# Half of wo with w_mod's FFN part ahead of the last K, w1 apart, w2 in five pieces, and a store of 128 partitions

## The chip, the core and the metric

The kernel runs on one core of one Trainium2 chip. The core has five engines that run their own instruction streams and meet through semaphores: PE (TensorE, matrix products; weight loads into it are shown apart as PEld), DVE (VectorE), ACT (ScalarE), POOL (GpSimd) and SP (SyncE), which here issues every DMA. The DMA engines move data between the chip's main memory and the on-chip memory (SBUF, 128 partitions); PE writes into PSUM, which also has 128 partitions.

The metric is the device time of one execution in microseconds (us), and the median over several runs. The profile is of one execution; its span runs from the first to the last instruction.

## What is computed

One decode step of a transformer block with conditioning, for a batch of 4, width 512, 32 query heads on 8 key/value heads ("groups", so 4 heads share a group), a window of 2048 cached positions, head size 128, and an FFN of width 1792. All values are 32-bit floats.

```python
def _A_ref(x, k_cache, v_cache, wq, wo):
    q = (x @ wq) ...
    k = jnp.repeat(k_cache[:, :, Sk - W:, :], rep, axis=1)
    v = jnp.repeat(v_cache[:, :, Sk - W:, :], rep, axis=1)
    scores = jnp.einsum("bhqd,bhkd->bhqk", q, k) * (Dh ** -0.5)
    p = _softmax(scores, axis=-1)
    o = jnp.einsum("bhqk,bhkd->bhqd", p, v)
    return o.transpose(0, 2, 1, 3).reshape(B, Sq, Hq * Dh) @ wo

def _B_ref(x, w1, w3, w2):
    return (_silu(x @ w1) * (x @ w3)) @ w2

mod = (_silu(c) @ w_mod).reshape(c.shape[0], 6, 1, -1)
sa, ca, ga, sb, cb, gb = ...
h = _layernorm(x) * (1 + ca) + sa
x = x + ga * _A_ref(h, A_k_cache, A_v_cache, A_wq, A_wo)
h = _layernorm(x) * (1 + cb) + sb
x = x + gb * _B_ref(h, B_w1, B_w3, B_w2)
```

Each of the eight groups needs 4 MB of K and 4 MB of V; the weights are wq and wo with 8 MB each, w_mod with 6 MB, and w1, w3 and w2 with 3.5 MB each. Every byte is used once.

## The kernel before

**Order and waits.** The function `block_kernel` lists all operations in one order. The class `Program` (lines 42 to 138) records each, works out from the places that it touches which earlier operations it has to wait for, and gives each engine its own part of that order with the waits as semaphores. An engine runs its part strictly in order. Every instruction is emitted on line 52, so the profile's line numbers don't tell them apart; the names of the tiles do. `do.mark()` splits the list in two parts with separate semaphores.

**The ring.** `ring` is one buffer of three slots of 8 MB (`slots[0]` to `slots[2]`), each of two halves of `HALF` = 8192 values for each partition (4 MB). All large loads go into it, in this order: w_mod's two attention columns (`w_mod_a`, slot 0), `xc_in` (x and c), wq (slot 1), then K and V of groups 0 to 7 in turn (`kv_in[g]`, 8 MB each, K in a slot's first half and V in its second), with wo (8 MB, slot 0) between group 6 and group 7. Group 7 comes as two loads, K and V, in slot 1. Then follow `w_mod_b` (slot 2: the four other columns of w_mod, 4 MB, and w1 behind them in the same load), w3 (slot 1, first half, in place of K7) and w2 (slot 1, second half, in place of V7) in four pieces, cut at chunks 0, 8, 12, 13 and 14 (`W2_CUTS`). The function `load` issues each on SP, which waits until the slot's former contents have been read.

**A group** (`group`, lines 306 to 326): PE multiplies the queries with K into four PSUM tiles `s_ps`; DVE takes the maximum of each (`mx`, then `nm`); PE turns the former group's output (`heads_out(g-1)`, tile `o_sb` times `pick`, into `oT`); ACT takes the exponent (`p_sb`), PE transposes it, DVE copies it to `pT`, PE multiplies it with V into `o_ps`; ACT scales it to `o_sb`.

**The end** (lines 338 to 403). After group 6, `project_out(0)` to `project_out(5)` multiply the finished heads with wo into `a_ps`; each call is four matmuls. Then comes group 7, `project_out(6)`, `heads_out(7)` and `project_out(7)`. ACT copies `a_ps` to `work`, and PE sums it into `attn`. `mod_columns` (16 matmuls of silu(c) with w_mod's four FFN columns) gives `mod_b`, which holds `ga`, `sh`, `cb1` and `gb`. DVE computes x1 = x + `ga` * `attn`; `norm` and `modulate` give h, which is transposed to `h2T`. `ffn_in` multiplies it with w1 (the gate, into `s_ps[0]`) and then with w3 (up, into `s_ps[1]`); each is 16 matmuls, a copy and four transposes. The product `hidT` meets w2 in 14 chunks of four matmuls, of which the last stands behind the mark. DVE multiplies with `gb` and adds x1 into `res`. Values for the four batch rows stand in every eighth partition, so the store takes `res[::8, :]`: 16 rows of 512 bytes.

Of the kernel before, what the change touches and what calls it, by code (L numbers as in the profile page):

```python
# [3 lines left out]
F32 = mybir.dt.float32  # L4
# [4 lines left out]
B, D, HQ, G, SK, DH, W, FF = 4, 512, 32, 8, 8192, 128, 2048, 1792  # L9
P = 128  # L10
R = HQ // G
# [1 line left out]
NC = 4  # L13
CHUNKS = [(c, j) for c in range(4) for j in range(4 if c < 2 else 3)]
NF = len(CHUNKS)
W2_CUTS = [0, 8, 12, 13, 14]
EPS = 1e-5
HALF = 8192

# [118 lines left out]
                nc.sync.sem_clear(done)  # L138


def block_kernel(nc, xc_in, w_mod_a, wq, kv_in, wo, w_mod_b, w3, w2, out):

# [1 line left out]
    do = Program(nc)  # L146

    def sb(name, *shape):
        return nc.alloc_sbuf_tensor(name, (P, *shape), F32).ap()

    def ps(name):
        return nc.alloc_psum_tensor(name, (P, 512), F32).ap()

    ring = sb("ring", 6 * HALF)
    slots = [ring[:, n * 2 * HALF : (n + 1) * 2 * HALF] for n in range(3)]
    s_ps = [ps(f"s_ps{t}") for t in range(NT)]
    banks = [ps(f"bank{n}") for n in range(2)]
    a_ps, o_ps = ps("a_ps"), ps("o_ps")
    turn = [0]

    def bank():
        turn[0] += 1
        return banks[turn[0] % 2]

    def load(dst, src):
        do("sync", "dma_start", dst, src)
        return dst

    def batch(t):

# [4 lines left out]
    x_sb, ct_sb = xc_sb[:, :P], xc_sb[:, P:]  # L175


    wma = load(slots[0][:, : w_mod_a.shape[1]], w_mod_a)
    load(xc_sb, xc_in)
    wq_t = load(slots[1], wq)  # L180
    kv = [None] * G
    kv[0] = load(slots[2], kv_in[0])
# [27 lines left out]
    oT = sb("oT", G, R, B)  # L210
# [9 lines left out]
    ss, ln, r0, ve, a, r = (sb(n, 1) for n in ("ss", "ln", "r0", "ve", "a", "r"))  # L220
# [26 lines left out]
    def mod_columns(wv, dst, n):  # L247

        pb = bank()
        for k in range(4):  # L250
            for j in range(4):
                do("tensor", "matmul", pb[32 * j : 32 * j + 32, : n * P], sc[:, k, :], wv[:, k, j, :], start=(k == 0), stop=(k == 3))
        do("vector", "tensor_copy", dst, pb[:, : n * P])
# [21 lines left out]
    for half in range(2):  # L275
# [4 lines left out]
        for i in range(R):  # L280
            src = qtp[:, i * P : (i + 1) * P].rearrange("p (g q) -> p g q", g=4)[:, :, ::8]
# [7 lines left out]

    def project_out(g):  # L290
        for i in range(R):
            do("tensor", "matmul", a_ps[32 * i : 32 * i + B, :], oT[:, g, i, :], wo_t[:, g, i, :], start=(g == 0), stop=(g == G - 1))

    mx, nm, ls, l, rl = (sb(n, m) for n, m in (("mx", NT), ("nm", 1), ("ls", NT), ("l", 1), ("rl", 1)))
    p_sb = [sb(f"p_sb{t}", 512) for t in range(NT)]
# [10 lines left out]
    def group(g):  # L306
        kt, vt = (kv[g][:, i * HALF : (i + 1) * HALF].rearrange("p (t b n) -> p t b n", t=NT, b=B) for i in range(2))
        for t in range(NT):
            for b in range(B):
                do("tensor", "matmul", s_ps[t][32 * b : 32 * b + 32, :], qT[:, g, b, :], kt[:, t, b, :], start=True, stop=True)  # L310
            do("vector", "reduce_max", mx[:, t : t + 1], s_ps[t], axis=AX.X)
        do("vector", "tensor_reduce", nm, mx, axis=AX.X, op=ALU.max, negate=True)
        if g:
            heads_out(g - 1)
        for t in range(NT):
            do("scalar", "activation", p_sb[t], s_ps[t], AF.Exp, bias=nm, accum_out=ls[:, t : t + 1])
            pt = bank()
            for c in range(NC):
                do("tensor", "transpose", pt[:, c * P : (c + 1) * P], p_sb[t][:, c * P : (c + 1) * P], ident)
            do("vector", "tensor_copy", pT[t], pt.rearrange("p (c b i) -> p b c i", b=B, i=32)[:, :, :, :R])  # L320
            for u in [t - 1] * (t > 0) + [t] * (t == NT - 1):
                for b in range(B):
                    do("tensor", "matmul", o_ps[32 * b : 32 * b + NC * R, :], pT[u][:, b].rearrange("p c r -> p (c r)"), vt[:, u, b, :], start=(u == 0), stop=(u == NT - 1))
        do("vector", "reduce_sum", l, ls, axis=AX.X)
        do("vector", "reciprocal", rl, l)
        do("scalar", "activation", o_sb, o_ps, AF.Copy, scale=rl)

    for g in range(G - 1):
        group(g)
        if g < 4:  # L330
            kv[g + 3] = load(slots[(g + 2) % 3], kv_in[g + 3])
        elif g == 4:
            wo_t = load(slots[0], wo).rearrange("p (g r n) -> p g r n", g=G, r=R)
        elif g == 5:
            kv[7] = slots[1]
            for i in range(2):
                load(kv[7][:, i * HALF : (i + 1) * HALF], kv_in[7][:, i * HALF : (i + 1) * HALF])
    wmb = load(slots[2][:, : w_mod_b.shape[1]], w_mod_b)
    for g in range(G - 2):
        project_out(g)  # L340
    group(G - 1)
    w3_t = load(slots[1][:, : w3.shape[1]], w3)
    w2_t = slots[1][:, HALF : HALF + w2.shape[1]]
    step = w2.shape[1] // NF
    for lo, hi in zip(W2_CUTS[:-1], W2_CUTS[1:]):
        load(w2_t[:, lo * step : hi * step], w2[:, lo * step : hi * step])
    project_out(G - 2)
    heads_out(G - 1)
    project_out(G - 1)

    do("scalar", "copy", work, a_ps)
    attn = bank()
    for j in range(4):
        do("tensor", "matmul", attn[32 * j : 32 * j + 32, :P], spread, work[:, j * P : (j + 1) * P], start=True, stop=True)

    mod_b = sb("mod_b", 512)
    ga, sh, cb1, gb = (mod_b[:, i * P : (i + 1) * P] for i in range(4))
    mod_columns(wmb[:, : 4 * 4 * 512].rearrange("p (k j i) -> p k j i", k=4, j=4), mod_b, 4)
    do("vector", "tensor_scalar_add", cb1, cb1, 1.0)
    x1, ag, tot2 = sb("x1", P), sq, sb("tot2", 1)  # L360
    do("vector", "tensor_mul", ag, attn[:, :P], ga)
    do("vector", "scalar_tensor_tensor", x1, ag, 1.0, x_sb, op0=ALU.mult, op1=ALU.add, accum_out=tot2)
# [4 lines left out]
    def ffn_in(ws, pg, g_sb):  # L367

        ws = ws.rearrange("p (k f) -> p k f", k=4)
        for k in range(4):
            for j in range(4):
                n = min(512, FF - 512 * j)
                do("tensor", "matmul", pg[32 * j : 32 * j + 32, :n], h2T[:, k, :], ws[:, k, j * 512 : j * 512 + n], start=(k == 0), stop=(k == 3))
        do("scalar", "copy", g_sb[:96], pg[:96])
        do("vector", "tensor_copy", g_sb[96:, :256], pg[96:, :256])
        gt = bank()
        for c in range(4):
            n, at = (128, c * 128) if c < 2 else (96, 256 + (c - 2) * 96)  # L380
            do("tensor", "transpose", gt[:, at : at + n], g_sb[:n, c * P : (c + 1) * P], ident[:n, :n])
        return gt[:, : NF * 32].rearrange("p (n i) -> p n i", i=32)[:, :, ::8]

    gate = ffn_in(wmb[:, 4 * 4 * 512 :], s_ps[0], p_sb[0])
    eg = sb("eg", NF, B)
    do("scalar", "activation", eg, gate, AF.Exp, scale=-1.0)
    do("vector", "tensor_scalar_add", eg, eg, 1.0)
# [5 lines left out]
    y_ps, y, res = s_ps[2], p_sb[2][:, :P], p_sb[3][:, :P]  # L393
    w2_t = w2_t.rearrange("p (n j i) -> p n j i", n=NF, j=4)
    for n in range(NF):
        if n == W2_CUTS[-2]:
            do.mark()
# [1 line left out]
            do("tensor", "matmul", y_ps[32 * j : 32 * j + 32, :P], hidT[:, n, :], w2_t[:, n, j, :], start=(n == 0), stop=(n == NF - 1))  # L399
    do("vector", "tensor_mul", y, y_ps[:, :P], gb)  # L400
    do("vector", "tensor_add", res, y, x1)
    do("sync", "dma_start", out, res[::8, :])
    do.emit()


def _layout(i):
    import numpy as np

    def a(t):
        return np.ascontiguousarray(t)  # L410

    k = i["A_k_cache"][:, :, SK - W :, :].reshape(B, G, NT, 512, DH)
    v = i["A_v_cache"][:, :, SK - W :, :].reshape(B, G, NT, NC, P, DH)
    wm = i["w_mod"].reshape(4, P, 6, 4, P)
    xc = np.zeros((4, 32, P + 16), np.float32)
    xc[:, ::8, :P] = i["A_x"].reshape(B, 4, P).transpose(1, 0, 2)
    xc = xc.reshape(P, P + 16)
    xc[:, P:] = i["c"].reshape(B, 4, P).transpose(2, 1, 0).reshape(P, 16)
    w2 = i["B_w2"].reshape(14, P, D)
    w_mod_b = a(wm[:, :, 2:].transpose(1, 0, 3, 2, 4)).reshape(P, 8192)  # L420
    w1 = a(i["B_w1"].reshape(4, P, FF).transpose(1, 0, 2)).reshape(P, 4 * FF)
    return {
        "xc_in": xc,
        "w_mod_a": a(wm[:, :, :2].transpose(1, 0, 3, 2, 4)).reshape(P, 4096),
        "wq": a(i["A_wq"].reshape(4, P, G, 512).transpose(1, 2, 0, 3)).reshape(P, 16384),
        "kv_in": np.concatenate([k.transpose(1, 4, 2, 0, 3).reshape(G, P, 8192), v.transpose(1, 4, 2, 0, 3, 5).reshape(G, P, 8192)], 2),
        "wo": a(i["A_wo"].reshape(G, R, P, D).transpose(2, 0, 1, 3)).reshape(P, 16384),
        "w_mod_b": np.concatenate([w_mod_b, w1], 1),
        "w3": a(i["B_w3"].reshape(4, P, FF).transpose(1, 0, 2)).reshape(P, 4 * FF),
        "w2": a(np.stack([w2[4 * j + c] for c, j in CHUNKS], 1)).reshape(P, NF * D),  # L430
    }
# [15 lines left out]
```

## Time and profile before

| what | value |
| --- | --- |
| median of 3 runs | 253.46 us |
| lowest and highest run | 251.55 and 253.53 us |
| time of the profiled execution | 253.12 us |
| its span | 251.7 us |
| mean granted clock of TensorE | 0.817 |
| loaded from memory | 101.26 MB |
| busy share of PE, DVE, ACT | 61%, 19%, 13% |

The profile shows busy time by engine, the span in 40 slices, the chain of work that ended last (followed back from the last instruction to what released it each time), and lists of instructions in order of time. In such a list a line gives start and length in us, engine, line, operation, output tile <- input tiles, the shapes, and how many instructions were merged; in brackets stands how long the engine was idle before and what ended that. Each 32-bit matmul appears as two instructions, so `project_out` shows as 8 and `mod_columns` as 32. PEclk is the granted clock of TensorE, 1.00 being full.

### The profile page before, as it was taken

To read this page: it belongs to the slowest core of one execution; us is meant where nothing else is said; L and a number is where in the kernel's file an instruction comes from. 1 tells how busy PE (TensorE), PEld (TensorE's weight loads), DVE (VectorE), ACT (ScalarE), POOL (GpSimd) and SP (SyncE) were. 2 spreads that over 40 slices of the span, in tenths; PEclk is the share of its full clock that TensorE was granted. 3 is DMA by queue.
4 is the path that set the end of the run, shared out by engine and by line. 5 is a ranking of instruction groups with operands and counts; after the bars stand their busy time and mean duration, and the time that the engine had idled before them with its cause. 6 is when DMAs were issued, how large, how long until landed. Compare 5 with 4: busy or idle time off the path is not lost.

```text
span 251.7 us, 2538 instructions
## 1 busy us (share of the span) xinstructions
PE 154.6 (61%) x1106; PEld 54.1 (21%) x1106; DVE 47.5 (19%) x155; ACT 33.4 (13%) x84; POOL 2.1 (1%) x9
## 2 busy tenths in 40 slices
PE   0340591279298489098298688278477768074975
PEld 0210130013033133023024124023111313011234
DVE  3220003041041041042032132023000500004021
ACT  2100000012004103104104104104100401000020
POOL 3000000000000000000000000000000000000000
PEclk9995589579867979869957979959959979757699
DMA  7999798998999989999899999999999999999700
GB/s 250 460 469 489 344 492 385 448 489 355 479 419 417 489 375 458 430 406 489 385 440 458 396 470 398 437 448 417 411 422 414 456 456 432 398 433 406 292 0 4
DMA packets 2778, 101.42 MB, mean 403 GB/s; under 512 B 320, under 2 KB 464, under 8 KB 720
## 3 DMA queue, kind: packets, MB, share of 16 engines
q1 hardware_dynamic: 2768, 101.27, 93.6%
q8 instruction: 8, 0.13, 0.2%
q14 instruction: 2, 0.02, 0.0%
HBM read 101.26 MB, written 0.01 MB: 402 GB/s over the span
## 4 chain that ended last, share of the span: by engine, by line
DMA 70%; PE 23%; DVE 3%; ACT 2%; issue 1%; SPq 0%; ACTq 0%; DVEq 0%
DMA ring<-kv_in 53%; DMA ring<-w_mod_b 17%; PE s_ps L52 12%; PE bank L52 7%; PE o_ps L52 5%; ACT p_sb L52 1%; DVE mx L52 1%; SPq L52 0%; DVE mod_b L52 0%; DVE p_sb L52 0%; DVE sq L52 0%; DVE nm L52 0%; DVE h L52 0%; DVE x L52 0%; DVE h2T L52 0%
## 5 line engine op out<-in xcount | busy, mean ns | idle before, releaser
L52 PE MATMUL s_ps<-ring,qT 128*32 128x512 f32 x256 | 44.6, 861 | 39.4 <-DMA ring<-kv_in 39.4
L52 DVE TENSOR_REDUCE mx<-s_ps 128x1 f32<-128x512 f32 x32 | 22.1, 692 | 89.4 <-PE s_ps L52 89.4
L52 PE MATMUL o_ps<-ring,pT 128*16 128x512 f32 x256 | 34.7, 639 | 2.9 <-DMA ring<-kv_in 2.9
L52 ACT ACTIVATE p_sb<-s_ps,nm 128x512 f32<-128x512 f32 x32 | 21.6, 686 | 101.2 <-PE bank L52 84.4
L52 PE MATMUL bank<-ident,p_sb 128*128 128x128 f32 (+1 forms) x136 | 23.8, 302 | 10.5 <-ACT p_sb L52 9.7
L52 PEld LDWEIGHTS s_ps<-ring,qT 128*32 128x32 f32 x256 | 10.1, 151 | 72.9 <-DMA ring<-kv_in 36.7
L52 PEld LDWEIGHTS bank<-ident,p_sb 128*128 128x128 f32 (+1 forms) x136 | 15.5, 150 | 31.7 <-ACT p_sb L52 14.2
L52 PE MATMUL s_ps<-ring,hT 128*32 128x512 f32 x64 | 9.3, 749 | 10.6 <-DMA ring<-wq 10.6
L52 DVE COPY pT<-bank 128x64 f32<-128x64 f32 x32 | 7.2, 225 | 44.2 <-PE bank L52 44.2
L52 PE MATMUL bank<-ring,sc 128*32 128x256 f32 (+1 forms) x64 | 10.0, 801 | 7.3 <-DMA ring<-w_mod_b 7.3
L52 PE MATMUL a_ps<-ring,oT 128*4 128x512 f32 x64 | 10.1, 778 | 5.6 <-DMA ring<-wo 5.3
L52 ACT ACTIVATE o_sb<-o_ps,rl 128x512 f32<-128x512 f32 x8 | 5.5, 688 | 43.3 <-PE o_ps L52 43.3
L52 PE MATMUL s_ps<-ring,h2T 128*32 128x512 f32 (+1 forms) x64 | 9.1, 662 | 0.4 <-DVE h2T L52 0.4
L52 PEld LDWEIGHTS bank<-pick,o_sb 128*128 128x128 f32 x64 | 7.7, 191 | 7.3 <-issue 6.3
L52 PE MATMUL bank<-pick,o_sb 128*128 128x16 f32 x64 | 8.5, 265 | 0.0
L52 PE MATMUL bank<-tot,avg 128*128 128x1 f32 x4 | 1.0, 312 | 11.5 <-DVE tot L52 9.9
L52 PEld LDWEIGHTS o_ps<-ring,pT 128*16 128x16 f32 x256 | 5.1, 96 | 12.5 <-issue 10.0
L52 ACT ACTIVATION_READ_ACCUMULATOR p_sb<-s_ps,nm 128x1 f32 x32 | 6.5, 203 | 0.0
L52 PEld LDWEIGHTS s_ps<-ring,hT 128*32 128x32 f32 x64 | 2.6, 135 | 16.7 <-issue 16.7
L52 DVE COPY qT<-bank 128x64 f32<-128x64 f32 x8 | 2.2, 276 | 20.6 <-PE bank L52 20.3
L52 PEld LDWEIGHTS bank<-ring,sc 128*32 128x32 f32 x64 | 2.8, 167 | 12.9 <-DMA ring<-w_mod_b 7.5
L52 ACT ACTIVATE work<-s_ps 128x512 f32<-128x512 f32 x2 | 1.2, 597 | 25.2 <-PE s_ps L52 21.8
(72 smaller groups left out, 42.3 us busy)
## 6 DMA issues: line engine op xcount, KB each, us to landing
ring<-kv_in SPq DMA_DIRECT2D x2, 4096.0 KB, 43.8
ring<-w_mod_b SPq DMA_DIRECT2D x1, 7680.0 KB, 42.8
ring<-w SPq DMA_DIRECT2D x1, 3584.0 KB, 32.6
ring<-w_mod_a SPq DMA_DIRECT2D x1, 2048.0 KB, 7.8
ring<-w SPq DMA_DIRECT2D x1, 2048.0 KB, 27.3
ring<-w SPq DMA_DIRECT2D x1, 1024.0 KB, 28.3
ring<-w SPq DMA_DIRECT2D x2, 256.0 KB, 28.2
ring<-kv_in SPq DMA_DIRECT2D x7, 44.4
```

Of the source, the lines that this page charges most:

```text
L52: op = Op(engine, lambda: getattr(getattr(self.nc, engine), method)(*args, **kw), [])
```

## The change

The host packs the weights in another way, and the loads of the end are cut and placed anew; what is computed stays the same.

- wo is split in two halves of 4 MB, for groups 0 to 3 and for groups 4 to 7. The first half and w_mod's four FFN columns are one array `wo_mod`, loaded into slot 0 at the place where wo was.
- After group 6, the second half of wo goes into slot 2's first half, and w1, now an array of its own, into its second half.
- Behind these loads PE has `project_out(0..3)` and then `mod_columns`, both ahead of group 7. `project_out(4..6)` moves behind group 7.
- w3 goes into slot 0's second half in two pieces, w2 into its first half in five (cut at chunks 0, 6, 10, 12, 13 and 14).
- The store takes all 128 partitions of `res`, 512 bytes each, into an output of 128 rows, and the host picks every eighth row.

```diff
-W2_CUTS = [0, 8, 12, 13, 14]
+W2_CUTS = [0, 6, 10, 12, 13, 14]
+W3_CUTS = [0, 1, 2]
...
-    def load(dst, src):
-        do("sync", "dma_start", dst, src)
-        return dst
+    def load(dst, src, cuts=(0, 1)):
+        step = src.shape[1] // cuts[-1]
+        for lo, hi in zip(cuts[:-1], cuts[1:]):
+            do("sync", "dma_start", dst[:, lo * step : hi * step], src[:, lo * step : hi * step])
+        return dst[:, : src.shape[1]]
...
-            do("tensor", "matmul", a_ps[32 * i : 32 * i + B, :], oT[:, g, i, :], wo_t[:, g, i, :], start=(g == 0), stop=(g == G - 1))
+            do("tensor", "matmul", a_ps[32 * i : 32 * i + B, :], oT[:, g, i, :], wo_t[g // 4][:, g % 4, i, :], start=(g == 0), stop=(g == G - 1))
...
         elif g == 4:
-            wo_t = load(slots[0], wo).rearrange("p (g r n) -> p g r n", g=G, r=R)
+            wom = load(slots[0], wo_mod)
         elif g == 5:
+            load(slots[1], kv_in[7], (0, 1, 2))
             kv[7] = slots[1]
-            for i in range(2):
-                load(kv[7][:, i * HALF : (i + 1) * HALF], kv_in[7][:, i * HALF : (i + 1) * HALF])
-    wmb = load(slots[2][:, : w_mod_b.shape[1]], w_mod_b)
-    for g in range(G - 2):
+    wo_t = [t.rearrange("p (g r n) -> p g r n", g=4, r=R) for t in (wom[:, :HALF], load(slots[2][:, :HALF], wo))]
+    w1_t = load(slots[2][:, HALF:], w1)
+    for g in range(4):
         project_out(g)
+
+    mod_b = sb("mod_b", 512)
+    ga, sh, cb1, gb = (mod_b[:, i * P : (i + 1) * P] for i in range(4))
+    mod_columns(wom[:, HALF:].rearrange("p (k j i) -> p k j i", k=4, j=4), mod_b, 4)
+    do("vector", "tensor_scalar_add", cb1, cb1, 1.0)
     group(G - 1)
-    w3_t = load(slots[1][:, : w3.shape[1]], w3)
-    w2_t = slots[1][:, HALF : HALF + w2.shape[1]]
-    step = w2.shape[1] // NF
-    for lo, hi in zip(W2_CUTS[:-1], W2_CUTS[1:]):
-        load(w2_t[:, lo * step : hi * step], w2[:, lo * step : hi * step])
-    project_out(G - 2)
+    w3_t = load(slots[0][:, HALF:], w3, W3_CUTS)
+    w2_t = load(slots[0][:, :HALF], w2, W2_CUTS)
+    for g in range(4, G - 1):
+        project_out(g)
     heads_out(G - 1)
     project_out(G - 1)
...
-    mod_b = sb("mod_b", 512)
-    ga, sh, cb1, gb = (mod_b[:, i * P : (i + 1) * P] for i in range(4))
-    mod_columns(wmb[:, : 4 * 4 * 512].rearrange("p (k j i) -> p k j i", k=4, j=4), mod_b, 4)
-    do("vector", "tensor_scalar_add", cb1, cb1, 1.0)
...
-    gate = ffn_in(wmb[:, 4 * 4 * 512 :], s_ps[0], p_sb[0])
+    gate = ffn_in(w1_t, s_ps[0], p_sb[0])
...
-    do("sync", "dma_start", out, res[::8, :])
+    do("sync", "dma_start", out, res)
...
+    wo = a(i["A_wo"].reshape(2, 4, R, P, D).transpose(0, 3, 1, 2, 4)).reshape(2, P, 8192)
...
+        "wo_mod": np.concatenate([wo[0], a(wm[:, :, 2:].transpose(1, 0, 3, 2, 4)).reshape(P, 8192)], 1),
+        "wo": wo[1],
+        "w1": a(i["B_w1"].reshape(4, P, FF).transpose(1, 0, 2)).reshape(P, 4 * FF),
...
-    out = nc.dram_tensor("out", (16, P), F32, kind="ExternalOutput").ap()
+    out = nc.dram_tensor("out", (P, P), F32, kind="ExternalOutput").ap()
...
-    y = r.results[0]["out"].reshape(4, B, P)
+    y = r.results[0]["out"].reshape(4, 32, P)[:, ::8]
```

More of the change, by code (lines that the diff above doesn't have):

```diff
@@ L138, in emit, with block_kernel @@
                 nc.sync.sem_clear(done)
-def block_kernel(nc, xc_in, w_mod_a, wq, kv_in, wo, w_mod_b, w3, w2, out):
+def block_kernel(nc, xc_in, w_mod_a, wq, kv_in, wo_mod, wo, w1, w3, w2, out):
     do = Program(nc)
@@ L175, in block_kernel @@
     x_sb, ct_sb = xc_sb[:, :P], xc_sb[:, P:]
-    wma = load(slots[0][:, : w_mod_a.shape[1]], w_mod_a)
+    wma = load(slots[0], w_mod_a)
     load(xc_sb, xc_in)
@@ L419, in _layout @@
     w2 = i["B_w2"].reshape(14, P, D)
-    w_mod_b = a(wm[:, :, 2:].transpose(1, 0, 3, 2, 4)).reshape(P, 8192)
-    w1 = a(i["B_w1"].reshape(4, P, FF).transpose(1, 0, 2)).reshape(P, 4 * FF)
+    wo = a(i["A_wo"].reshape(2, 4, R, P, D).transpose(0, 3, 1, 2, 4)).reshape(2, P, 8192)
     return {
@@ L426, in _layout @@
         "kv_in": np.concatenate([k.transpose(1, 4, 2, 0, 3).reshape(G, P, 8192), v.transpose(1, 4, 2, 0, 3, 5).reshape(G, P, 8192)], 2),
-        "wo": a(i["A_wo"].reshape(G, R, P, D).transpose(2, 0, 1, 3)).reshape(P, 16384),
-        "w_mod_b": np.concatenate([w_mod_b, w1], 1),
+        "wo_mod": np.concatenate([wo[0], a(wm[:, :, 2:].transpose(1, 0, 3, 2, 4)).reshape(P, 8192)], 1),
+        "wo": wo[1],
+        "w1": a(i["B_w1"].reshape(4, P, FF).transpose(1, 0, 2)).reshape(P, 4 * FF),
         "w3": a(i["B_w3"].reshape(4, P, FF).transpose(1, 0, 2)).reshape(P, 4 * FF),
```

## The prediction

> **What bounds the kernel now.** I read the page's slices first, then the chain of work that ended last, then the timeline of the last 70 us, then the DMA issues.
>
> ```profile
> core 0 of [0], span 251.7 us
> DMA  7999798998999989999899999999999999999700
> ```
>
> ```profile
> by line: DMA ring<-kv_in 53.3%; DMA ring<-w_mod_b 17.0%; PE s_ps L52 12.0%; PE bank L52 6.5%; PE o_ps L52 4.6%; ACT p_sb L52 1.4%; issue 0.9%; DVE mx L52 0.8%; SPq L52 0.5%; DVE mod_b L52 0.4%; DVE p_sb L52 0.2%; DVE sq L52 0.2%; DVE nm L52
> ```
>
> The first is the share of the DMA engines in 40 slices of 6.3 us, in tenths: full in every slice up to the 38th, then empty. Up to about 239 us the kernel is a stream of loads; behind it lies a tail without traffic. The second is the chain by what stood on it: 53.3 and 17.0% are loads, the last of them `w_mod_b`. The row of times has 253.12 us for this execution, so 1.42 us lie outside its span of 251.7; the median of the three runs is 253.46, 0.34 us above. The sum below is made against 253.12.
>
> The SP queue (start, length, what) and, from the list of DMA issues, the time from issue to landing at each row's end:
>
> ```profile
> 0.73 0.38 SPq L52 DMA_DIRECT2D ring<-w_mod_a  x1
> 1.17 0.42 SPq L52 DMA_DIRECT2D xc_sb<-xc_in  x1
> ...
> 179.00 0.33 SPq L52 DMA_DIRECT2D ring<-w_mod_b  x1
> 197.65 13.37 SPq L52 DMA_DIRECT2D ring<-w  x5
> 249.94 0.55 SPq L52 DMA_DIRECT2D out<-p_sb  x1
> ```
>
> ```profile
> ring<-w_mod_b SPq DMA_DIRECT2D x1, 7680.0 KB, 42.8
> ring<-w SPq DMA_DIRECT2D x1, 3584.0 KB, 32.6
> ring<-w_mod_a SPq DMA_DIRECT2D x1, 2048.0 KB, 7.8
> ...
> ring<-w SPq DMA_DIRECT2D x2, 256.0 KB, 28.2
> ...
> xc_sb<-xc_in SPq DMA_DIRECT2D x1, 72.0 KB, 7.5
> ...
> out<-p_sb SPq DMA_DIRECT2D x1, 8.0 KB, 1.7
> ```
>
> `w_mod_b` holds w_mod's four FFN columns and w1 together. It was issued at 179.00 and landed 42.8 us later, at 221.8, since it stands in the queue behind V of the last group. What PE did around it:
>
> ```profile
> 184.27 8.05 PE L52 MATMUL a_ps<-ring,oT 128*4 128x512 f32 x48 [5.30 <-DMA ring<-wo]
> 193.98 3.64 PE L52 MATMUL s_ps<-ring,qT 128*32 128x512 f32 x32 [1.66 <-DMA ring<-kv_in]
> ...
> 203.77 1.91 PE L52 MATMUL o_ps<-ring,pT 128*16 128x512 f32 x8 [2.85 <-DMA ring<-kv_in]
> ...
> 208.29 1.91 PE L52 MATMUL o_ps<-ring,pT 128*16 128x512 f32 x16
> 210.02 1.04 PE L52 MATMUL a_ps<-ring,oT 128*4 128x512 f32 x8
> 211.06 1.07 PE L52 MATMUL bank<-pick,o_sb 128*128 128x16 f32 x8
> 212.40 1.04 PE L52 MATMUL a_ps<-ring,oT 128*4 128x512 f32 x8 [0.27 <-DVE oT L52]
> 214.14 0.43 PE L52 MATMUL bank<-work,spread 128*32 128x128 f32 x8 [0.71 <-ACT work L52]
> 221.82 6.35 PE L52 MATMUL bank<-ring,sc 128*32 128x512 f32 x32 [7.25 <-DMA ring<-w_mod_b]
> ```
>
> ```profile
> 228.26 0.69 DVE L52 COPY mod_b<-bank 128x512 f32<-128x512 f32 x1 [15.91 <-PE bank L52]
> 228.98 0.23 DVE L52 TENSOR_SCALAR mod_b<-mod_b 128x128 f32<-128x128 f32 x1
> 229.12 0.28 DVE L52 TENSOR_TENSOR sq<-bank,mod_b 128x128 f32<-128x128 f32 x1
> ```
>
> At 184.27 `wo` has landed and 24 matmuls (48 instructions, each matmul being two) of `project_out` run; at 193.98 K of group 7 lands, at 203.77 V. At 214.57 (214.14+0.43) the attention output is in `attn`. Then PE waits 7.25 us for `w_mod_b`, runs 32 instructions of `mod_columns` at a low clock, and only at 229.12 does DVE multiply `attn` by `ga`. So between 214.57 and 229.12 the path is one late load and the work on it, and from 221.82 to the end no engine waits for a load again: 29.9 us of PE, DVE and ACT, longer than what is left to load.
>
> **When the loads will land.** Landing times follow one another as the sizes do. K to V of group 7: 9.79 us (193.98 to 203.77) for 4096 KB. V to `w_mod_b` (PE starts at 221.82): 18.05 us for 7680 KB. w3: 197.65+32.6 = 230.25, so 8.47 us for 3584 KB. w2's four pieces: SP's five issues end at 197.65+13.37 = 211.02, the last began some 0.4 before, and 210.6+28.2 = 238.8, so 8.55 us for another 3584 KB. Everything lands at about 2.4 us per 1024 KB, whatever it was cut into. The bytes of the changed kernel are the same, and so is the order up to V of group 7 (203.75). Then half of `wo` (4096 KB, 9.7 us) lands at 213.45, w1 (8.45) at 221.9, the halves of w3 at 226.1 and 230.35, and w2 at 238.8 as before. The SP waits that change: half of `wo` waits for K6's scores instead of V6's products, w1 waits where `w_mod_b` waited (179.00), w3 for `mod_columns` and w2 for `project_out(0..3)`, both done by 194 (below) where w3 went out at 197.65 before. All come some 19 us or more before the stream reaches them, so nothing behind them on SP is late.
>
> **The change part by part.**
>
> *Half of wo and w_mod ahead of group 7.* The 8 MB load keeps its place and size, so it lands at 184.27. On PE, 32 instructions of `project_out(0..3)` and 32 of `mod_columns` replace 48. The stage's rows:
>
> ```profile
> 184.00:189.00 5.00, 4.73 (x24) 0.85 (x28) 0.00 (x0) 0.00 (x0) 0.00 (x0) 0.50 0.97 419
> 189.00:192.00 3.00, 3.00 (x28) 0.54 (x20) 0.00 (x0) 0.00 (x0) 0.00 (x0) 0.87 1.10 464
> ```
>
> 24 start in the first 4.73 us at clock 0.50, then it rises. So the 32 end near 189.9 (8 more by the second row, 28 in 3.00), and 32 more of 512 columns take 3.64 at full clock (the row at 193.98): 193.5. K lands at 193.98, so group 7 starts on time. At half clock `mod_columns` would take 6.35 and end at 196.3, 2.3 us late; the 2.85 us that PE waits for V at 203.77 cover it, and if that cover were gone, 2.3 us is the price, itself still under the wait for `wo` below. What is queued behind `mod_columns` is group 7 alone. DVE's copy and add (0.69+0.23) end at 194.5, before the first quarter of the 3.64 us of scores, which the first maximum waits for. Cost taken: 0. Gain: 221.78 to 229.12 leaves the path.
>
> *The other half of wo behind V.* This is the new wait: group 7's products end near 210.0, and PE then waits until 213.45. Queued behind that wait on PE are `project_out(4..6)` (24 instructions), `heads_out(7)`, which needs no load, and `project_out(7)`; ACT's `work` waits for them. The 24 cost 3.1 us at full clock (three times the 1.04 of the row at 210.02) or 4.7 at half clock (24 in 4.73). I take 4.7: after 2.85 us without work 8 `o_ps` instructions took 1.91 (at 203.77), where later 16 took as long (208.29), while after 1.66 us (193.98) the clock stayed up; 3.4 us is nearer the first. They end at 218.15.
>
> The Trainium skill (TensorE: Matmul & The Clock Gate, Part 1) lets the clock fall after an idle window of about 3.4 us and rise after as long a busy one, the windows running freely. By that rule a wait of 3.4 us stands just at the edge, and the sum would be either this one or the first rival's; here 2.85 us sufficed.
>
> *From there to the end.* From `heads_out`'s start to the end of `attn` it took 3.51 us (211.06 to 214.57): 221.65. `mod_b` is long there. The next rows give the rest:
>
> ```profile
> 233.87 5.45 PE L52 MATMUL s_ps<-ring,h2T 128*32 128x512 f32 x32 [0.38 <-DVE h2T L52]
> ...
> 240.62 3.63 PE L52 MATMUL s_ps<-ring,h2T 128*32 128x512 f32 x32
> ...
> 245.96 3.26 PE L52 MATMUL s_ps<-ring,hidT 128*32 128x128 f32 x112 [0.35 <-DVE hidT L52]
> ```
>
> From DVE's product at 229.12 to the gate's matmuls at 233.87: 4.75, plus 0.1 to start: 226.5 (w1 has landed at 221.9). From gate to up: 6.75, with its cold start (5.45 for the matmuls, 3.63 for the same number warm): 233.25 (w3 whole at 230.35). From up to w2's product: 5.34: 238.6. From there to the end of the span 5.74: 244.35. PE comes to the last chunk of w2 some 3 us after 238.6; it has landed at 238.8. So loads are no longer what ends last, but nearly: the stream has 2.9 us of slack.
>
> *w3 in two, w2 in five, w1 apart: three more loads.* Four pieces of w2 took 0.08 us more than one of w3 (8.55 against 8.47), so three more cost 0.1 on a stream with 2.9 us of slack: 0 on the path. From above each is bounded by the store's 1.7 us, a load that finds an empty queue (rival 2). Nothing is gained either: gate and up come after their loads in both cuttings.
>
> *The store.* 16 rows of 512 B took 1.7 us from issue to landing, 0.55 of that issuing. For 128 rows: `xc_in`, 128 rows of 576 B, landed at 1.17+7.5 = 8.67, 0.14 us behind `w_mod_a` (0.73+7.8 = 8.53). From below, -0.2 (a load of 128 rows was issued in 0.33 at 179.00, not 0.55); from above, +0.6 (the 128 rows of 2 KB of a 256 KB piece, at 2.4 us per 1024 KB). I take +0.15, by the row nearest in shape: 244.5.
>
> **The sum.** 221.78 to 229.12 leaves the path; it now starts from 213.45 with 4.7+3.51+0.1 to the same point, 7.36 us earlier, and the store gives back 0.15: 251.7 - 7.2 = 244.5, and with 1.42 around it 245.9, rounded to 246.0. That is 2.8% below 253.12; a run like the median would be at 246.2.
>
> **The rivals.**
>
> 1. *The clock stays up.* If PE doesn't slow in the 3.4 us wait, 24 instructions take 3.1 or a little less and the gate may start warmer (5.45 to 3.63). Then 1.6 to 3.4 us go: PE would come to the last chunk of w2 when it lands, so the stream limits it: 238.8, 0.3 for the last chunk, 2.5 (251.7 less 245.96+3.26) to the end, 0.15 for the store: 241.75, or 243.2. For it: the row at 193.98. Against: the row at 203.77, and the gate's 5.45 at 233.87, though PE had worked until 228.2 and in bursts since.
>
> 2. *Each further load drains the queue.* If a load began only when its forerunner had landed, the price of each is that of the store, 1.7 us with hardly a byte. Three: 5.1, the stream ends at 243.9 and the span at 246.85: 248.3. Against it: four pieces of w2 took 8.55 us where one of w3 took 8.47. The Trainium skill (DMA: Bandwidth & Descriptors, Anatomy of one DMA) puts about 2.0 us of fixed cost on each DMA; by that, an estimate from the page, the time would be some 0.9 us more. It speaks against cutting, but the trace disagrees for queued loads.
>
> 3. *The queue doesn't keep its order* (slower). Now up to nine loads are queued at once behind V where there were six. If half of `wo` advanced side by side with what follows, it would land not at 213.45 but with w1 and w3: at 221.9 the end is 8.45 us later, 254.4, about no change; with w3's halves at 230.35 it is 262.9. It decides from 223.1 on: there the time is 1% above before. Against it: `w_mod_b` (issued 179.00) stood behind K and V, and w3 (197.65) behind V and `w_mod_b`, and each landed by its own size after the one before.
>
> 4. *The change doesn't do what it says*: were `mod_columns` in effect still late, its load landing near 221.8 as `w_mod_b` did, there would be no gain: 253. Nothing in the profile speaks for it; the load ahead is the one of `wo` in size and place.
>
> **How the numbers follow.** Forecast 0.62 (244.6 to 247.6: the store from -0.2 to +0.6, half clock lasting through `heads_out` for 1 us more); rival 1 0.20 (243.0 to 244.6); rival 2 0.08; rival 3 0.05, half of it slower by over 1%; rival 4 and other ways to no change 0.05. The time is the forecast's, 246.0. Within 1% is about what a measurement of this kernel can't tell from no change. Faster: 0.62+0.20+0.08 = 0.90; slower 0.03; within 1% 0.07. The range leaves out rivals 3 and 4 and the far ends: 243.2 to 248.2. Runs of before lie between 251.55 and 253.53, which widens nothing beyond that.
>
> **What would show it.** In the changed kernel: `mod_columns` from about 190 to 193.5 and group 7's scores at 194; `project_out(4..6)` starting at 213.4 behind a wait on DMA of `wo` of about 3.4 us, 4.7 us long; gate near 226.5, up near 233, w2's product near 238.6; no wait on w1, w3 or w2; last packets near 239; the chain naming `wo` as its last load. Wrong if `wo` lands late, if the up or w2 product waits for its load, if the stream ends past 241.7, or if the store takes over 2.5 us.

## The result, and the profile after

| | before | changed |
| --- | --- | --- |
| median, us (6 runs of each) | 252.33 | 244.56 |
| lowest and highest | 251.1 and 253.53 | 243.52 and 246.18 |
| profiled execution, us | 253.12 | 243.92 |
| its span | 251.7 | 242.5 |

The ratio of the runs is 0.97, with a 95% interval of 0.9645 to 0.9755. The time fell by 3%; 246.0 was forecast, in a range of 243.2 to 248.2. Sums below compare the two spans, 9.2 us apart.

The slices of the changed kernel (share of the DMA engines, in tenths, each slice 6.06 us) and, from the page, the chain by what stood on it:

```profile
core 0 of [0], span 242.5 us
DMA  7997979898989898989898999999999999999992
```

```profile
DMA ring<-kv_in 56%; DMA ring<-wo 18%; PE s_ps L53 12%; PE bank L53 4%; PE o_ps L53 3%; PE a_ps L53 2%; ACT p_sb L53 1%; SPq L53 1%; DVE mx L53 0%; DVE sq L53 0%; DVE p_sb L53 0%; ACT work L53 0%; DVE h L53 0%; DVE x L53 0%; DVE xc L53 0%
```

The stream of loads now fills all slices but the last. The last load on the chain is no longer `w_mod_b` but the second half of `wo`. PE's timeline (start, length, operation, in brackets the idle time before and its end) shows how each stage moved:

```profile
184.18 5.65 PE L53 MATMUL a_ps<-ring,oT 128*4 128x512 f32 x32 [5.98 <-DMA ring<-wo_mod]
189.65 3.61 PE L53 MATMUL bank<-ring,sc 128*32 128x512 f32 x32
193.88 3.64 PE L53 MATMUL s_ps<-ring,qT 128*32 128x512 f32 x32 [0.62 <-DMA ring<-kv_in]
...
209.16 1.91 PE L53 MATMUL o_ps<-ring,pT 128*16 128x512 f32 x16
213.31 2.76 PE L53 MATMUL a_ps<-ring,oT 128*4 128x512 f32 x24 [2.23 <-DMA ring<-wo]
215.99 1.06 PE L53 MATMUL bank<-pick,o_sb 128*128 128x16 f32 x8
...
224.12 6.18 PE L53 MATMUL s_ps<-ring,h2T 128*32 128x512 f32 x32 [0.38 <-DVE h2T L53]
...
231.59 3.63 PE L53 MATMUL s_ps<-ring,h2T 128*32 128x512 f32 x32
...
236.93 3.27 PE L53 MATMUL s_ps<-ring,hidT 128*32 128x128 f32 x112 [0.35 <-DVE hidT L53]
```

`mod_columns` (32 instructions, `bank<-ring,sc`) runs from 189.65 to 193.26, before K of group 7 lands, and costs nothing there. Half of `wo` lands at 213.3, where 213.45 was forecast; PE had waited 2.23 us. In DVE's timeline the product of `attn` with `ga` starts at 219.56 instead of 229.12:

```profile
219.56 0.29 DVE L53 TENSOR_TENSOR sq<-bank,mod_b 128x128 f32<-128x128 f32 x1 [2.29 <-PE bank L53]
```

So the path gained 9.56 us up to this product. From there to the gate it took 4.56 us instead of 4.75 (gain 0.19), from gate to up 7.47 instead of 6.75 (loss 0.72), and from up to the end of the span 10.91 instead of 11.08 (gain 0.17, the store in it). Together: 9.2 us.

The clock explains both the stage that was cheaper than forecast and the one that was dearer. In these rows, the column behind the five engines is the granted clock:

```profile
213.50:217.00 3.50, 3.50 (x32) 1.40 (x24) 0.00 (x0) 0.00 (x0) 0.00 (x0) 1.00 1.07 459
217.00:222.00 5.00, 2.29 (x21) 0.86 (x20) 1.35 (x7) 0.82 (x2) 0.00 (x0) 1.00 0.92 393
222.00:226.00 4.00, 2.36 (x15) 0.93 (x19) 1.29 (x6) 0.23 (x2) 0.00 (x0) 0.56 0.99 419
226.00:232.00 6.00, 5.21 (x35) 1.44 (x31) 0.48 (x2) 0.80 (x2) 0.00 (x0) 0.73 1.01 429
```

In the 24 instructions of `project_out(4..6)` it is 1.00. When DVE works on `norm` and `modulate` PE has little to do (2.29 us of 5 between 217 and 222), and from 222 to 226, where the gate begins, the clock is 0.56 on average: the gate's 32 instructions take 6.18 us, and up takes 3.63 for as many.

### The profile page after: what moved, and what is told of

Read it like the earlier page. It is cut to its first block, busy times and chain, and to the rows that moved or that the text cites. A ratio compares the mean times of both kernels' runs of the same rounds, so it can differ in the third digit from the quotient of the medians.

```text
span 242.5 us, 2543 instructions
## 1 busy us (share of the span) xinstructions
PE 147.2 (61%) x1106; PEld 52.2 (22%) x1106; DVE 47.6 (20%) x155; ACT 33.4 (14%) x84; POOL 2.1 (1%) x9
## 4 chain that ended last, share of the span: by engine, by line
DMA 74%; PE 21%; DVE 2%; ACT 1%; issue 1%; SPq 1%; DVEq 0%; ACTq 0%
DMA ring<-kv_in 56%; DMA ring<-wo 18%; PE s_ps L53 12%; PE bank L53 4%; PE o_ps L53 3%; PE a_ps L53 2%; ACT p_sb L53 1%; SPq L53 1%; DVE mx L53 0%; DVE sq L53 0%; DVE p_sb L53 0%; ACT work L53 0%; DVE h L53 0%; DVE x L53 0%; DVE xc L53 0%
## 5 line engine op out<-in xcount | busy, mean ns | idle before, releaser
L53 PE MATMUL s_ps<-ring,qT 128*32 128x512 f32 x256 | 43.0, 833 | 43.0 <-DMA ring<-kv_in 43.0
L53 PE MATMUL o_ps<-ring,pT 128*16 128x512 f32 x256 | 33.8, 624 | 2.9 <-DMA ring<-kv_in 2.9
L53 PE MATMUL bank<-ident,p_sb 128*128 128x128 f32 (+1 forms) x136 | 22.6, 290 | 10.4 <-ACT p_sb L53 9.8
L53 PEld LDWEIGHTS bank<-ident,p_sb 128*128 128x128 f32 (+1 forms) x136 | 14.7, 144 | 30.8 <-ACT p_sb L53 14.9
L53 PE MATMUL s_ps<-ring,hT 128*32 128x512 f32 x64 | 8.5, 693 | 10.5 <-DMA ring<-wq 10.5
L53 PE MATMUL a_ps<-ring,oT 128*4 128x512 f32 x64 | 9.4, 730 | 8.5 <-DMA ring<-wo_mod 6.0
L53 PE MATMUL s_ps<-ring,h2T 128*32 128x512 f32 (+1 forms) x64 | 9.8, 705 | 0.4 <-DVE h2T L53 0.4
L53 PE MATMUL bank<-ring,sc 128*32 128x256 f32 (+1 forms) x64 | 7.2, 612 | 0.0
L53 PEld LDWEIGHTS a_ps<-ring,oT 128*4 128x4 f32 x64 | 1.6, 96 | 15.5 <-DMA ring<-wo_mod 6.9
```

The lines of the kernel that those rows point to most:

```text
L53: op = Op(engine, lambda: getattr(getattr(self.nc, engine), method)(*args, **kw), [])
```

## The experiments

The theory is that the end hangs on when half of `wo` lands (213.3), on the 29.2 us of PE, DVE and ACT behind it, and on which stretch of these finds PE's clock down; the stream of loads ends shortly before it would decide. Rivals: that the end hangs on the stream, that the finer pieces matter, or that the early load alone matters and not the moved work. Each kernel is the changed one with the edit shown; the kernel before ran beside all of them.

### The changed kernel again

No edit; run twice, on two occasions.

> The changed kernel once more, for the clock. In its profile half of wo landed at 213.3, PE had waited 2.23 us, the 24 instructions behind took 2.76 us (full clock) and the gate's 32 took 6.18 (half clock for most). Theory (the tail hangs on the landing of half of wo and on which stretch of it PE's clock is down): landing again within 0.5 us of 213.3, but the slow stretch may lie elsewhere: 24 instructions between 2.7 and 4.8 us, gate between 3.6 and 6.4, and the span between 240.5 and 245 accordingly. Rival (runs differ by how fast the loads go): the landing moves by 1 us or more and the span with it, the slow stretches being the same. Time 243.5 to 246.2.

> The changed kernel a third time, beside the next kernel on the same chip. Theory and rival alike: 243.5 to 246.2, median near 245; its runs spread by over 1 us, since PE's clock falls in one stretch or another.

Medians of 245.32 (244.54 to 246.36) and 243.8 (243.67 to 244.83), so three medians of the same kernel, with the 244.56 above, lie 1.5 us apart. PE's rows of the first repetition:

```profile
194.76 3.64 PE L53 MATMUL s_ps<-ring,qT 128*32 128x512 f32 x32 [0.89 <-DMA ring<-kv_in]
...
214.18 2.76 PE L53 MATMUL a_ps<-ring,oT 128*4 128x512 f32 x24 [2.13 <-DMA ring<-wo]
...
225.51 6.01 PE L53 MATMUL s_ps<-ring,h2T 128*32 128x512 f32 x32 [0.39 <-DVE h2T L53]
```

Half of `wo` landed at 214.18, 0.9 us later than in the first profile of this kernel (213.31), since the stream as a whole ran later by that (K at 194.76 instead of 193.88). The wait and the two stretches behind it were the same: 2.76 at full clock, the gate 6.01 at low clock. So this run is nearer to the rival: the slow stretch lay where it was, and the landing moved, by just under the 1 us that the rival named. The span is 243.7, so 0.9 of the 1.2 us are the stream's. The second repetition has the same picture: `wo` at 213.85, 2.76 us, and a gate of 6.19. What made runs of 246 us was not profiled.

### The order of the two loads behind V

```diff
-    wo_t = [... (wom[:, :HALF], load(slots[2][:, :HALF], wo))]
     w1_t = load(slots[2][:, HALF:], w1)
+    wo_t = [... (wom[:, :HALF], load(slots[2][:, :HALF], wo))]
```

> The changed kernel with the two loads behind V in the other order: w1 first, then half of wo; nothing else is altered. Theory (the tail hangs on the landing of half of wo): wo lands at 221.8 instead of 213.3 (3584 KB at 2.4 us per 1024 KB), and the end comes 8 to 11 us later (PE idles 11 us, so the 24 instructions behind run at half clock, up to 2 us more): span 250.5 to 253.5, about the time of before or 1% less. Rival (the end hangs on the stream, and wo has slack): no change, span 242 to 244.

253.76 us (253.29 to 255.13), 1.0077 of before (1.0042 to 1.0111): the whole gain is gone, with not one byte or instruction altered.

```profile
221.83 5.18 PE L53 MATMUL a_ps<-ring,oT 128*4 128x512 f32 x24 [10.36 <-DMA ring<-wo]
...
235.59 6.00 PE L53 MATMUL s_ps<-ring,h2T 128*32 128x512 f32 x32 [0.38 <-DVE h2T L53]
```

Half of `wo` lands at 221.8, as worked out from its forerunner's size, 8.5 us later. PE has then idled for 10.36 us, and the 24 instructions take 5.18 instead of 2.76. The span grew by 11.3 us (253.8 less 242.5): 8.5 of landing, 2.4 of `project_out`, and 0.4 elsewhere. That is 0.3 above the span that was expected, and the profiled run is the slowest of the eight; between the medians of the two kernels, taken on different occasions, lie 9.2 us. The end hangs on this landing, and the rival that it hangs on the stream is out: all bytes, and their order behind these two loads, are the same, and only the end moved.

### mod_columns back behind attn, its load early

```diff
-    mod_columns(wom[:, HALF:]..., mod_b, 4)
-    do("vector", "tensor_scalar_add", cb1, cb1, 1.0)
     group(G - 1)
...
         do("tensor", "matmul", attn[32 * j : 32 * j + 32, :P], ...)
+    mod_columns(wom[:, HALF:]..., mod_b, 4)
+    do("vector", "tensor_scalar_add", cb1, cb1, 1.0)
```

> The changed kernel with mod_columns and the addition of 1.0 back where they were, behind attn; w_mod still lands with the first half of wo, some 30 us before. Theory (between attn and DVE's product stands then the work alone: 3.6 to 6.4 us of PE, 0.69 and 0.23 of DVE, about 5 to 7 us, of which the gate gives back up to 2.5 us because PE's clock is up when it begins): end 2.5 to 6 us later, span 245 to 249. Rival 1 (only the load had to be early, since the work is hidden by something): no change. Rival 2 (the whole gain of the change comes from the work moved ahead): span 250 or more.

258.33 us (257.94 to 259.06). In program order w3 now lands over w_mod before `mod_columns` reads it, so `mod_columns` computes with w3's values and waits for w3:

```profile
226.02 3.64 PE L53 MATMUL bank<-ring,sc 128*32 128x512 f32 x14 [4.91 <-DMA ring<-w]
230.31 2.91 PE L53 MATMUL bank<-ring,sc 128*32 128x512 f32 x18 [0.65 <-DMA ring<-w]
```

It starts at 226.02 and goes on at 230.31, when the two halves of w3 have landed. It tells nothing on the question, but dates the halves: 226.0 and 230.3, where 226.1 and 230.35 were worked out. The next kernel puts w3 in slot 1, in place of K7, as the kernel before did:

```diff
-    w3_t = load(slots[0][:, HALF:], w3, W3_CUTS)
+    w3_t = load(slots[1][:, :HALF], w3, W3_CUTS)
```

> mod_columns behind attn again, but with w3 loaded into slot 1's first half (in place of K7, as before the change) so that it doesn't land over w_mod, which is what made mod_columns wait for w3 in the former attempt. w_mod has landed at 184. Theory: only the work stands between attn (219.5 or, with a colder project_out, 221.2) and DVE's product: 3.6 us of PE, since the clock is up, and 0.92 of DVE, some 4.6 us in all; the gate then starts with the clock up, 3.6 instead of 6.2 us. Net 2 to 4 us later than the changed kernel: span 244 to 246.5. Rival 1 (only the load had to be early): no change, 242 to 243.5. Rival 2 (the gain is in the moved work): 249 or more.

248.65 us (247.88 to 250.3), span 246.6: 4.1 us over the changed kernel's 242.5 and just above the expected range; the medians of this occasion are 4.85 us apart (243.8 for the changed kernel). PE's rows, then DVE's:

```profile
219.50 3.62 PE L53 MATMUL bank<-ring,sc 128*32 128x512 f32 x32
...
228.70 5.65 PE L53 MATMUL s_ps<-ring,h2T 128*32 128x512 f32 x32 [0.38 <-DVE h2T L53]
```

```profile
224.05 0.28 DVE L53 TENSOR_TENSOR sq<-bank,mod_b 128x128 f32<-128x128 f32 x1
```

With nothing to wait for, `mod_columns` takes 3.62 at full clock, and DVE's product starts at 224.05, 4.5 us after the changed kernel's 219.56, as expected. The second half of the expectation failed: the gate isn't helped by the work ahead of it; it takes 5.65 us, since some 5 us of `norm` and `modulate` lie between. Of the 4.5 us, 0.2 are a later landing of `wo`; the gate took 0.5 less, and what lies around it 0.1 more, which makes the 4.1. Of the 9.2 us in the spans, 5.1 are there without the move of the work (251.7 to 246.6), and that move adds 4.1; by the medians of this occasion (252.87 for the kernel before) it is 4.2 and 4.85. So about half of the gain comes from either, and the first rival is out. The second, that the gain is in the moved work alone, set 249 or more for the span: the four runs have 246.6, 246.7, 248.0 and 249.0, so one of them reaches it and three do not.

### The pieces of w3 and w2

Fewer, as before the change:

```diff
-W2_CUTS = [0, 6, 10, 12, 13, 14]
-W3_CUTS = [0, 1, 2]
+W2_CUTS = [0, 8, 12, 13, 14]
+W3_CUTS = [0, 1]
```

> The changed kernel with w3 in one load and w2 in four, cut as before. Theory (the end hangs on the landing of half of wo, and the pieces lie beside it): up starts when the gate is done, w2's product waits for no load, span as the changed kernel's but for the clock, median within 0.5%. Rival 1 (each load costs 1.7 us on the stream): last packets 3.4 us earlier than 239. Rival 2 (the finer pieces are what lets up and w2's product start early): a wait of PE on w3 or w2 appears and the time is 1 us or more longer.

And many more (`W2_CUTS = list(range(15))`, `W3_CUTS = list(range(9))`):

> The changed kernel with w3 in eight pieces and w2 in fourteen: fifteen loads more. Theory (a queued load costs next to nothing: 0.03 us by w2's four pieces against w3's one): the stream ends within 0.5 us of 239, and the time stays within 1% of the changed kernel's, unless SP, which stood 7.4 us at the last piece of w2 in the changed kernel, falls so far behind that the stream runs dry. Rival (each queued load drains the queue, 1.7 us): the stream ends 10 us or more after 239, PE waits for w3 and w2, span 250 or more.

Fewer: 244.23 us (243.5 to 246.21) beside 245.32 of the changed kernel on the same occasion, with intervals of the ratio to before that overlap (0.9662 to 0.9742, and 0.9697 to 0.9764). Up starts when the gate is done and nothing waits for a load. The last piece lands at 238.9 (194.69, its issue, and 44.2), in the changed kernel at 239.0 (195.57 and 43.4), so two loads fewer don't end the stream earlier by more than 0.1 us. Many: 245.06 (244.28 to 245.55). The last rows of PE's timeline with many pieces:

```profile
236.88 3.15 PE L53 MATMUL s_ps<-ring,hidT 128*32 128x128 f32 x104 [0.35 <-DVE hidT L53]
240.24 0.43 PE L53 MATMUL s_ps<-ring,hidT 128*32 128x128 f32 x8 [0.21 <-DMA ring<-w]
```

Only the last chunk of w2 waits, 0.21 us, until its piece lands at 240.2. With the changed kernel's cuts it lands at 239.0, or at 239.3 by PE's wait in the kernel below with the clock held up. So fifteen more loads cost the stream 0.9 to 1.2 us, 0.06 to 0.08 each, more than the 0.5 us in all that was expected. That each drains the queue (1.7 us) is out; that the cut brings anything is not seen either.

### The store

```diff
-    do("sync", "dma_start", out, res)
+    do("sync", "dma_start", out, res[::8, :])
```

(and an output of 16 rows)

> The changed kernel with the store of 16 rows (res[::8, :]) as before. Theory: issue 0.55 instead of 0.35 us and landing 1.7 instead of 1.6 after issue, so the end behind the last DVE operation is 0.1 to 0.2 us longer; the median within 0.5% of the changed kernel's. Rival (the wide store costs, 0.15 us as predicted or more): the end gets shorter by 0.15 to 0.6 us.

245.13 us (244.07 to 246.33), beside 245.32: no difference in the whole. SP's row and the list of DMA issues, first for 16 rows, then for the changed kernel's 128:

```profile
241.18 0.56 SPq L53 DMA_DIRECT2D out<-p_sb  x1
```

```profile
out<-p_sb SPq DMA_DIRECT2D x1, 8.0 KB, 1.8
```

```profile
240.91 0.35 SPq L53 DMA_DIRECT2D out<-p_sb  x1
```

```profile
out<-p_sb SPq DMA_DIRECT2D x1, 64.0 KB, 1.6
```

From its issue to the end of the span the store takes 1.82 us with 16 rows (243.0 less 241.18) and 1.59 with 128 (242.5 less 240.91). Eight times the bytes are not slower: the issue is 0.2 us shorter, and that is the whole difference.

### Holding PE's clock up

Matmuls of `ident` by `ident` into `s_ps[3]`, which nothing reads, in PE's gaps: two behind `attn`, two and five in `norm`, one behind the transpose:

```diff
+    def warm(n):
+        for _ in range(n):
+            do("tensor", "matmul", s_ps[3][:, :P], ident, ident, start=True, stop=True)
...
+    warm(2)
-    norm(x1, tot2)
+    norm(x1, tot2, 2, 5)
     modulate(cb1, sh)
     h2T = transposed("h2T")
+    warm(1)
```

> The changed kernel with ten further matmuls of ident by ident into s_ps[3], which nothing reads, put in the gaps of PE between attn and the gate (2, 2, 5 and 1). Theory (the gate's 6.18 us is PE's clock falling in the gaps of norm and modulate): PE's clock stays near 1.00 from 217 us to the gate, the gate's 32 instructions take 3.6 to 4.5 us, and w2's product is then bounded by its last load near 239: span 240.5 to 241.5, time 1 to 2 us below the changed kernel's, some 0.5%. Rival (the clock falls anyway, or the gate is slow for another reason, such as reading w1 beside the loads): gate 5.4 to 6.4 us, no gain, or 0.2 to 0.5 us lost to the added matmuls.

244.07 us (243.09 to 244.55), where the changed kernel had 245.32.

```profile
213.29 4.46 PE L53 MATMUL a_ps<-ring,oT 128*4 128x512 f32 x24 [3.05 <-DMA ring<-wo]
...
225.66 3.63 PE L53 MATMUL s_ps<-ring,h2T 128*32 128x512 f32 x32 [0.16 <-DVE h2T L53]
```

The gate takes 3.63 us instead of 6.2, as the theory has it. But the span is 242.8, not the 240.5 to 241.5 that were expected. In this execution `project_out(4..6)` found the clock down: PE had idled 3.05 us and the 24 instructions took 4.46. That is the case which the prediction had taken for the likely one. And the store took 2.5 us from issue to landing where it took 1.6 in the changed kernel, for a reason that is not known. The next kernel adds seven such matmuls to the wait for `wo`:

```diff
+    warm(7)
     for g in range(4, G - 1):
         project_out(g)
```

> The kernel with matmuls in the gaps of norm, with seven more of them behind group 7's products, in the wait for half of wo. Theory: with the clock up both in project_out (2.8 instead of up to 4.5 us) and in the gate (3.6 us) the path from wo's landing is 2 us shorter than the changed kernel's, the product with w2 now waits for its last pieces (PE 0.5 to 2 us longer there), and the stream sets the end: span 241.0 to 242.0, time 242.5 to 243.5, 0.5 to 1% below the changed kernel's. Rival (the stream has slack left): w2's product waits for nothing, and the span falls to 240.5 or less. Rival (the clock falls in the wait all the same): as the kernel with ten matmuls.

> The kernel with seventeen added matmuls (seven in the wait for wo, ten in the gaps of norm) again. Theory (the clock's falls cost the changed kernel 1 to 2 us, and with them gone the stream sets the end): 243.2 to 243.8, runs within 0.5 us of each other, below the changed kernel's median on the same chip by 0.8 to 2 us. Rival (chips or chance made the difference): within 0.5 us of the changed kernel's median.

243.37 us on both occasions (243.24 to 243.48, and 243.19 to 243.44), beside 243.8 of the changed kernel on the second; the ratios to before are 0.9664 (0.963 to 0.9698) and 0.9643 (0.961 to 0.9675). PE's rows of the first of the two:

```profile
213.40 2.76 PE L53 MATMUL a_ps<-ring,oT 128*4 128x512 f32 x24 [0.18 <-DMA ring<-wo]
...
224.06 3.63 PE L53 MATMUL s_ps<-ring,h2T 128*32 128x512 f32 x32 [0.16 <-DVE h2T L53]
...
234.32 1.52 PE L53 MATMUL s_ps<-ring,hidT 128*32 128x128 f32 x48 [0.35 <-DVE hidT L53]
236.68 1.08 PE L53 MATMUL s_ps<-ring,hidT 128*32 128x128 f32 x32 [0.84 <-DMA ring<-w]
237.94 1.04 PE L53 MATMUL s_ps<-ring,hidT 128*32 128x128 f32 x24 [0.19 <-DMA ring<-w]
239.30 0.43 PE L53 MATMUL s_ps<-ring,hidT 128*32 128x128 f32 x8 [0.31 <-DMA ring<-w]
```

`project_out` 2.76, gate 3.63. The product with w2 starts at 234.32, 2.6 us earlier than in the changed kernel, and then waits three times for its pieces, the last until 239.3. Now the stream sets the end, at a span of 242.0, just 0.5 below the 242.5 of the changed kernel's first profile. The path through PE and the stream are that near to each other.

The profile of the second occasion shows the same by accident: there the clock fell before the gate in spite of the added matmuls, and the gate took 3.93 us and began later:

```profile
224.63 3.93 PE L53 MATMUL s_ps<-ring,h2T 128*32 128x512 f32 x32
...
239.37 0.43 PE L53 MATMUL s_ps<-ring,hidT 128*32 128x128 f32 x8 [0.40 <-DMA ring<-w]
```

The product with w2 began 0.9 us later than on the first occasion (235.19), and the span was 242.1 all the same. So the added matmuls don't hold the clock up in every execution.

On that occasion, the only one with both kernels, the medians lie 0.43 us apart. That is less than the 0.8 to 2 us expected, and within the 0.5 us that the rival had named; the intervals of the ratios overlap. Yet all six runs (to 243.44) lie below all six of the changed kernel (from 243.67), so a small gain is likely and its size is not shown. What is plain is the spread: 1.2 to 2.7 us among the changed kernel's six runs on each occasion, 0.3 us over these twelve.

## Why the prediction was right

**The tail hangs on the last load that starts it.** Right. Half of `wo` landed at 213.3 (213.45 forecast), and the swap of two loads took the whole gain back. The second rival (each load drains the queue) would have needed 1.7 us for a load that cost 0.08 at most; the third (no order in the queue) is answered by landings that follow the sizes in each kernel, w3's halves at 226.0 and 230.3 among them; the fourth (`mod_columns` still late) by its start at 189.65. The 2.0 us that the prediction sets beside the second rival are given in the Trainium skill (DMA: Bandwidth & Descriptors, Anatomy of one DMA) for DMAs that GpSimd issues; the queued loads here, which SP issues, cost 0.08 at most.

**The work ahead of group 7 costs nothing.** Right: 189.65 to 193.26, forecast 189.9 to 193.5; K's scores began at 193.88.

**project_out behind the new wait at half clock, 4.7 us.** This step was mis-sized: 2.76. The prediction set PE's wait at 3.4 us, because it let group 7's products end at 210.0 as before. They ended at 211.07, since the clock was low for longer in front of them; the second eight, before and then in the changed kernel:

```profile
206.65 1.13 PE L52 MATMUL o_ps<-ring,pT 128*16 128x512 f32 x8
```

```profile
206.57 1.91 PE L53 MATMUL o_ps<-ring,pT 128*16 128x512 f32 x8
```

So the wait was only 2.23 us, and the clock stayed up. Of nine profiles with the loads in this order and PE empty in the wait, seven had waits of 2.02 to 2.48 us and 2.76 us for the 24 instructions; two had 3.05 and 3.15 us and 4.46. With the seven added matmuls in the wait it was 2.76.

The traces show why such waits come out one way or the other. Read in stretches of 0.25 us between 180 and 240 us, the granted clock of each of the thirteen profiles changes only at points that lie whole multiples of 3.41 us apart (in the changed kernel near 188.3, 202.0, 208.8, 222.4 and 229.3), and where these points lie differs from one execution to the next. Call the 3.41 us between two neighbouring points a window. Two windows around the wait, in the kernel with ten added matmuls and then in the changed kernel (the first engine column is PE's busy time, and the clock stands behind the five engines):

```profile
210.43:213.84 3.41, 0.55 (x8) 0.22 (x12) 0.00 (x0) 0.57 (x1) 0.00 (x0) 1.00 0.96 414
213.84:217.25 3.41, 3.41 (x24) 0.51 (x12) 0.00 (x0) 0.00 (x0) 0.00 (x0) 0.50 0.96 412
```

```profile
208.80:212.21 3.41, 2.27 (x20) 0.56 (x18) 0.45 (x3) 0.69 (x1) 0.00 (x0) 1.00 0.99 426
212.21:215.62 3.41, 2.31 (x24) 0.54 (x24) 0.00 (x0) 0.00 (x0) 0.00 (x0) 1.00 0.98 420
```

In the first kernel the wait took up most of one window, and the clock was 0.50 in the next; in the changed kernel the wait fell on two windows with over 2 us of work in each, and the clock stayed at 1.00. Over the thirteen profiles, a window at full clock with up to 1.3 us of PE's busy time was followed by half clock every time, and one with 2.5 us or more never; between the two both occur. So the prediction's step failed in going by the length of the wait alone, and that it failed in this direction was partly chance: it was right for two of the nine. The Trainium skill (TensorE: Matmul & The Clock Gate, Part 1) has the clock fall after one idle window of about 3.4 us, its windows running freely; the trace agrees on the length, 3.41 us, but the window need not be idle: 0.55 us of work in it did not hold the clock up, nor did 1.19 us between 219.04 and 222.45 in the changed kernel.

**The gate with its cold start as before.** Right in kind, short in size: 6.18 instead of 5.45, and 0.72 us lost from gate to up.

**The store, +0.15.** Wrong in sign and small: the stage from its issue to the end became 0.2 us shorter (1.76 before, 251.7 less 249.94, and 1.59 now).

**Three more loads, 0; 2.9 us of slack of the stream.** Right in kind. The last piece lands at 239.0 where 238.8 was worked out, and PE came to it near 239.9 (236.93 and 3 us), earlier than forecast, so the slack was 0.9 us.

The sum: 2.0 us less in `project_out` (2.7 instead of 4.7), 0.3 from up to the end, the store in it, 0.2 on the landing and DVE's start behind it, and 0.2 between DVE's product and the gate, against 0.72 more in the gate, give 242.5 instead of 244.5.

The median, 244.56, lies 1.4 below the forecast. It is inside the range, but just under 244.6, where the prediction had drawn the line between its own case and rival 1 (the clock stays up). In the profiled run half of that rival came true: the clock stayed up in `project_out` and not in the gate. That the total is no further off is partly luck, since one miss made up for a third of the other. With the clock up in both stretches the time was 243.37, and rival 1 had 243.2.

## What to carry to other kernels

Where a stream of loads fills nearly all of the time, ask which load the last dependent work starts from, and put that load as early as the buffers allow, with everything that only feeds later steps behind it; swapping two loads was worth 9 us here. Work whose inputs can be had early goes into an earlier wait of its engine. When the path behind the last load and the stream end within a microsecond or two of each other, shortening either alone gives only their difference. How long PE waits does not by itself tell the clock behind the wait, so a forecast needs both cases, with their prices.

## What the runs showed of the hardware

SP stood in an issue when nine loads were under way. The issue of w2's last piece took 7.38 us in the changed kernel, until 202.95, about when V landed (PE's products with V start at 203.68); before it, nine loads were under way. With six loads instead of eight behind `wo` no issue took long: the last five went out in 2.23 us, with seven under way at the last. With twenty-three the first long issue also came with nine under way, and took 8.46 us, from 194.50 to 202.96. From w1's issue to the end of the last it was 52.93 us, of which SP waited 12.2 behind the first issue for `mod_columns` to have read w_mod; the 256 KB pieces landed 10.7 us after their issue instead of some 43. What frees SP is not settled: the next long issue there ended at 211.3, 2 us before `wo` landed. SP's rows of the changed kernel, of the one with few and the one with many pieces, and the issues of the 256 KB pieces in the changed kernel and with many pieces:

```profile
195.57 7.38 SPq L53 DMA_DIRECT2D ring<-w  x1
```

```profile
192.90 2.23 SPq L53 DMA_DIRECT2D ring<-w  x5
```

```profile
178.16 52.93 SPq L53 DMA_DIRECT2D ring<-w  x23
```

```profile
ring<-w SPq DMA_DIRECT2D x2, 256.0 KB, 43.4
```

```profile
ring<-w SPq DMA_DIRECT2D x14, 256.0 KB, 10.7
```

The stream lost at most the 1.2 us given above. It would matter where something else waits behind those loads on SP.
